# A quarter of w_out moved up in the load order, longer filler matmuls, and a planner that knows how many loads the queue holds

## The chip, the cores and the metric

The kernel runs on one core of a Trainium2 chip. The metric is the time of one execution on the device, in microseconds: 212.72 us as the median of three runs (212.54 to 212.77). The profiled execution took 212.52 us, and its trace has a span of 210.7 us from the first to the last instruction. Five engines work side by side, each in the order in which its instructions were written: TensorE (PE, matrix products), VectorE (DVE), ScalarE (ACT), GpSimd (POOL) and SyncE (SP). Loads issued from GpSimd go through one software queue of the DMA engines; SyncE has a hardware queue.

## The reference

Two stages follow each other. The first is a recurrent attention with a decaying state (4 batches, 8 heads, 768 steps, 64 columns for each head):

```python
    gamma = 1.0 - 2.0 ** (-5.0 - np.arange(H, dtype=np.float32))
    scale = 1.0 / np.sqrt(D)
    for t in range(S):
        state = gamma[None, :, None, None] * state + np.einsum('bhd,bhe->bhde', k[:, :, t], v[:, :, t])
        y[:, :, t] = scale * np.einsum('bhd,bhde->bhe', q[:, :, t], state)
```

The second takes the rows of y as 3072 tokens of 512 columns and puts them through two matrix products (w_in is 512 x 2048, w_out is 2048 x 512) with a gate between them:

```python
    h = x @ w_in
    g = h * np.cos(h)
    return (g @ w_out).astype(np.float32)
```

## The kernel before

**Tiling.** The recurrence is done in chunks of 128 steps: inside a chunk as a masked product of q and k with v, between chunks through the state. A *slot* is one chunk of two batches; there are twelve, numbered 0 to 11 in the order of `ORDER`. Two slots make a *group* of 512 tokens, and there are six groups. For one slot the work is: load q, k and v (`load`, L273); scale q and v and convert k to bf16 (`conv_q` L308, `conv_v` L312, `conv_k`); transpose q and k on TensorE (`t_mm`, L337) or, from slot 6 on, by DMA; scores (`a_mm`, L363 and L366); mask them on VectorE (`a_mask`, L372); y from the state and from the scores (`y1_mm` L428, `intra` L414, `y_first` L395); the state's update (`s_mm`, L460); and a copy of y into the token tile `xt` (`y_copy`). `copy` at L297 and L299 is a helper for all plain copies, so many different copies have its lines.

**The second stage.** A unit of the first product gives 128 columns of h for 512 tokens (`f_mm`, L472, four matmuls) or 256 columns of h for the 256 tokens of one slot (`h_mm`, L493, eight matmuls of 256 columns, called a half-width unit here). ScalarE takes the cosine (`f_cos`, L480), VectorE multiplies (`f_mul` L484, `h_mul` L501). The second product (`o_mm`, L517) adds up 128 tokens' output in one PSUM bank in four parts, part r with quarter r of w_out. PSUM has eight banks: seven go around in a list (`Banks`), one holds the state. An output block holds its bank from its first part to its last.

**Loads.** A q, k or v load of a slot is one "merged" transfer of 512 KB for both batches. In `LOADS`, "q3" is slot 3's q, "Q1" and "K1" are loads of slot 1 that convert on the way, "w1" is the second quarter of w_in (512 columns), "w0a" and "w0b" are halves of the first quarter, and "o0" to "o3" are the quarters of w_out (`load_w_out`, L289). All of them are issued by GpSimd in the order of the list (each waits for the one before to be issued). A new transfer of the queue also waits for the semaphore of the transfer eight places earlier.

**The order of the work.** For the first eight slots' loads and the first six slots' attention the order is not written by hand. `Plan` is a list scheduler that runs when the kernel is built: each operation has engines on which it may run, a cost in microseconds, operations that it follows, a rank (a small one goes first), and tokens that it takes and gives back ("bank", "cos" for the cosine buffers, "sem" for the queue's eight semaphores[...]). For loads it keeps one running time of the queue, adding size over rate and a lag for each load. `jitter` adds a random number from 0 to 4 to every rank, drawn from `SEED`. The instructions are then written in the order of the planned starts (`emit`), and the chip takes them in that order on each engine, whether or not the planned times come true. Between 4.2 and 18 us of the plan, where TensorE would have to wait longer than one filler takes, the planner puts in a filler, `idle_mm`: a matmul on zeros into a free bank, which keeps TensorE's clock up. The first seven, ahead of the plan, have 512 columns; those of the plan have 256.

**After the plan**, from about 65 us, a loop over the groups interleaves `f_mm` of one group, `o_mm` of the group before and the attention of slots 6 to 11.

The lines of the edit: the seed (L163), the engines for slot 2's scaling (`CQ` for q, `CD` for v, L589, used at L639 and L649), the token table (L592), the load list and `LAG` (L601 to L604), the merged loads' tokens (L609 to L611) and the filler given to `plan.run` (L801).

Of the kernel before, what the change touches and what calls it, by code (L numbers as in the profile page):

```python
# [29 lines left out]
class Plan:  # L30
# [16 lines left out]
    def add(self, engines, cost, fn, after=(), rank=0.0, take=(), give=(), mode=None,  # L47
            spare=0, mb=0.0, rate=0.0, lag=0.0, name=""):
        op = dict(engines=engines, cost=cost, fn=fn, after=[a for a in after if a], rank=rank,
                  take=take, give=give, mode=mode, spare=spare, mb=mb, rate=rate, lag=lag,  # L50
                  n=len(self.ops), start=None, done=None, free=None, name=name)
        self.ops.append(op)
        return op
# [106 lines left out]
            op["fn"](op["eng"])  # L160


SEED, JIT, HOLD = 41, 4.0, "PD"  # L163
HALF0, SPARE, RF, RM, COLD = 4, 1, 40.0, 40.0, 5.2


# [1 line left out]
def kernel(  # L168
# [10 lines left out]
    B, H, S, D = q.shape  # L179
# [86 lines left out]
    def load(eng, p, names):  # L266

        bp, c = divmod(ORDER[p], NC)
        for n in names.split():
            t, src = SRC[n[0].lower()]  # L270
            if len(n) == 1:
                t = (qb(p) if n == "Q" else kb(p)) if n in "QK" else t[p % PRE]
                eng.dma_start(  # L273
                    out=t.rearrange("p b h d -> p (b h) d"),
                    in_=src[ds(2 * bp, 2), :, ds(c * C, C), :].rearrange(
                        "b h t d -> t (b h) d"))
            else:
                b = int(n[1])
                eng.dma_start(
                    out=t[p % PRE][:, b],  # L280
                    in_=src[2 * bp + b, :, ds(c * C, C)].rearrange("h t d -> t h d"))

    def load_w_in(lo, n):
        nc.gpsimd.dma_start(
            out=w_in_sb[:, :, ds(lo, n)],
            in_=moe_w_in[:, ds(lo, n)].rearrange("(i p) f -> p i f", p=128))

    def load_w_out(r):
        nc.gpsimd.dma_start(  # L289
            out=w_out_sb[:, ts(r, 4), :],  # L290
            in_=moe_w_out[ts(r, 512), :].rearrange("(f p) m -> p f m", p=128))
# [252 lines left out]
    def idle_mm(e, n=1):  # L544
        bank = banks.take()
        nc.tensor.matmul(bank[:, : 256 * n].rearrange("p (n t) -> p n t", n=n),  # L546
                         lhsT=zero[:, :128], rhs=zero.unsqueeze(1).to_broadcast([128, n, 256]),
                         start=True, stop=True)
        banks.give(bank)
# [15 lines left out]
        out=dist.rearrange("p (a b) -> p a b", a=8),  # L565
# [16 lines left out]
    for i in range(7):  # L582
# [3 lines left out]
    PL = 6  # L586
    ASEP = 4
    MERGE = 4
    CQ, CD = "D", "D"  # L589
    SPLIT = {(1, 1, 0), (0, 1, 1)}  # L590
    HM, HCQ, HCV = "q2", "", ""
    plan = Plan({"bank": 7, "cos": 3, "sem": 8, "out": 4, "port": 1}, 6.5)  # L592
    add = plan.add
    SB2 = {"D": (0.33, 0.42), "A": (0.49, 0.585)}
    TT = {"D": (0.6, 0.69), "P": (1.03, 1.05)}
# [2 lines left out]
    prev = None  # L598
    at = lambda tm: dict(start=0.0, free=0.0, done=tm, lat=0.0)
    ld["q", 0, 0], ld["q", 0, 1], ld["k", 0, 0], ld["k", 0, 1] = map(at, (3.9, 5.0, 7.4, 7.4))  # L600
    LOADS = ["Q1", "K1", "v0", "v1", "w0a", "w0b", "w1", "w2", "q2", "k2", "w3a", "v2", "w3b", "q3", "k3", "v3",  # L601
             "o0", "o1", "o2", "o3", "q4", "k4", "v4", "q5", "k5", "v5", "q6", "k6", "v6",
             "q7", "k7", "v7"]
    LAG = {}  # L604
    pend = []
    for i, x in enumerate(LOADS):
        if x[0] in "qkvQK":
            p = int(x[1:])
            o = add("P", 1.2, lambda e, p=p, n=x[0]: load(nc.gpsimd, p, n),  # L609
                    [("issued", prev)] if prev else [], 50 + i if p < 7 else 45,  # L610
                    [("sem", 1)], [("sem", 1)], mb=524288e-6, rate=330e-3, name=x)  # L611
            ld[x[0].lower(), p, 0] = ld[x[0].lower(), p, 1] = o
            if p >= PRE:
                pend.append((o, x[0], p - PRE))
        elif x[0] == "w":
            r, w = int(x[1]), len(x) == 3
            lo = 512 * r + (256 if x[2:] == "b" else 0)
            o = add("P", 0.76, lambda e, lo=lo, n=256 if w else 512: load_w_in(lo, n),
                    [("issued", prev)], 50 + i, [("sem", 1)], [("sem", 1)],
                    mb=(524288e-6 if w else 1048576e-6), rate=(390e-3 if w else 415e-3),  # L620
                    lag=LAG.get(x, 0.0), name=x)
            for f in range(lo // 128, lo // 128 + (2 if w else 4)):
                ld["w", f] = o
        else:
            r = int(x[1])
            o = add("P", 0.76, lambda e, r=r: load_w_out(r), [("issued", prev)], 50 + i,
                    [("sem", 1)], [("sem", 1)], mb=1048576e-6, rate=415e-3, name=x)
            ld["o", r] = o
        prev = o
    T = {}  # L630
    G = lambda *k: T.get(k)
    for p in range(PL + 2):
        c = ORDER[p] % NC

        for b in range(2):
# [18 lines left out]
            if p < 2:  # L654
                T["cv", p, b] = add("AD"[b], SB2, lambda e, p=p, b=b: raw_v(p, b, e), [ld["v", p, b]],
                                    10 * p + 2.5 + b, [("port", 1)] if b else [], [("port", 1)] if b else [],
                                    name="rv%d%d" % (p, b))
        old = [G("a", p - NB, b) for b in range(2)] + [G("y", p - NB, b) for b in range(2)]
        if p < DMA_T:

            for u in range(2):
# [3 lines left out]
                                            name="e%s%d%d" % (x, p, u))  # L665
# [7 lines left out]
                else:  # L673
                    tq = tk = add("E", 0.45, lambda e, p=p, u=u: (t_mm(p, u, 0), t_mm(p, u, 1)),
                                  cq + ck, 10 * p + 1, [("bank", 1)], (), "full",
                                  name="t%d%d" % (p, u))
# [4 lines left out]
        else:  # L681
            for w, x in enumerate("qk"):
                T["dt", p, w] = add("S", (1.3, 4.6), lambda e, p=p, w=w: dma_t(p, w),
                                    [T["c" + x, p, 0], T["c" + x, p, 1]] + old, 10 * p,
                                    name="dt%d%d" % (p, w))
# [5 lines left out]
        elif p < ASEP:  # L691
            for u in range(2):
                T["a", p, u] = add("E", 0.225, lambda e, p=p, u=u: a_mm(p, u), kq[u], 10 * p + 2,
                                   [("bank", 2)], (), "row" if p < 2 else "quad",
                                   name="a%d%d" % (p, u))
# [4 lines left out]
        for u in range(2):  # L700
            for b in range(2):
                if (p, b, u) in SPLIT:
                    o = add("A", (0.49, 0.585), lambda e, p=p, b=b, u=u: a_save(p, b, u),
                            [T["a", p, u]], 0, (), [("bank", 1)],
                            name="ms%d%d%d" % (p, b, u))
                    T["m", p, b, u] = add("P", (1.1, 1.2), lambda e, p=p, b=b, u=u: a_late(p, b, u),
                                          [o], 0, [("port", 1)], [("port", 1)],
                                          name="ml%d%d%d" % (p, b, u))
# [16 lines left out]
        else:  # L725

            a_next = MERGE <= p < PL
            def y(e, p=p, a_next=a_next):
# [8 lines left out]
                if not a_next:  # L737
# [3 lines left out]
                    name="y%d" % p)  # L741
# [9 lines left out]
        for b in range(2):  # L751
# [4 lines left out]
                                name="yc%d%d" % (p, b))  # L756
# [8 lines left out]
        for u in units:  # L765
# [4 lines left out]
            else:  # L770
# [5 lines left out]
                     name="cos%s%d.%d" % u)  # L776
            T["mul", u] = add("D", (0.6, 0.69), mul, [c1], RM, (), [("bank", 1), ("cos", 1)],
                              name="mul%s%d.%d" % u)
# [19 lines left out]
        add("A", (0.49, 0.585), lambda e, j=j: (o_out(0, j, e), o_dma(0, j)), [T["o", j, 3]], 300, (),  # L798
            [("bank", 1)], name="oc%d" % j)
    plan.jitter(SEED, JIT)  # L800
    plan.run({"S": 2.5, "P": 3.2, "A": 5.5, "D": 3.6, "E": 4.2}, COLD, 0.6, (4.2, 18.0, 0.12, idle_mm), HOLD)  # L801
    plan.emit()

    for p in (PL + 2, PL + 3):
# [83 lines left out]
```

## Time and profile before

| what | value |
|---|---|
| time, median of 3 | 212.72 us |
| span of the trace | 210.7 us |
| TensorE clock granted | 1.00 in all stages |
| busy: TensorE, VectorE, ScalarE, GpSimd | 97%, 52%, 55%, 37% |
| bytes read and written in HBM | 27.26 MB and 6.29 MB |
| software queue | 15.47 MB written, first landing 7.05 us, last 62.44 us |
| fillers (L546) | 62, of them 55 with 256 columns |
| merged load, issue on GpSimd | 1.19 us |
| merged load, from landing to landing | 1.52 us |
| quarter of w_out, from landing to landing | 2.45 to 2.60 us |

How to read it: the shares are means over a head in which loads arrive (to 62 us) and a body in which all is loaded. Landing times of single loads are those at which the last of the sixteen landing signals of a load stands in the trace. In the views of the profile, "x8" is a count, the number after a start time is a duration in us, and brackets give the idle time of the engine ahead of the instruction, with what ended it.

### The profile page before, as it was taken

How to read it: one execution, taken by the hardware profiler on the slowest of the kernel's cores; microseconds unless marked ns; L12 is line 12 of the kernel's file. 1: busy time of each engine (PE TensorE's matmuls, PEld its weight loads, DVE VectorE, ACT ScalarE, POOL GpSimd, SP SyncE). 2: the span in 40 equal slices, each digit the busy share in tenths (PEclk: the TensorE clock that was granted, in tenths of full speed). 3: DMA queues.
4: the chain of work that ended last, by engine and by line, in shares of the span. 5: the costliest groups of instructions: out<-in, count | busy, mean ns of one | idle time of the engine just before them, and what ended most of it. 6: DMA issues, size and time to landing. Idle time of an engine off the chain costs nothing.

```text
span 210.7 us, 4885 instructions
## 1 busy us (share of the span) xinstructions
PE 203.6 (97%) x2046; PEld 111.8 (53%) x2046; DVE 109.7 (52%) x189; ACT 115.4 (55%) x193; POOL 78.0 (37%) x82
## 2 busy tenths in 40 slices
PE   7998989998999999999999999999999999999993
PEld 3776456686765545445446445445444444444462
DVE  5464999876755646537437447447442333333000
ACT  7776768387575447547547547545545554553120
POOL 8889969979998007007007007000000000000000
PEclk9999999999999999999999999999999999999999
DMA  7999999999987399999994501501101101110221
GB/s 120 202 250 235 298 323 216 215 337 344 344 259 164 103 219 240 240 208 255 117 256 143 145 30 39 151 12 56 50 3 50 50 3 50 50 50 18 84 83 68
DMA packets 57496, 32.05 MB, mean 152 GB/s; under 512 B 46593, under 2 KB 51969, under 8 KB 57473
## 3 DMA queue, kind: packets, MB, share of 16 engines
q0 software_dynamic: 14352, 15.47, 33.3%
q1 hardware_dynamic: 42976, 16.13, 30.4%
q8 instruction: 16, 0.26, 0.5%
q10 hardware_dynamic: 144, 0.13, 0.2%
q14 instruction: 8, 0.06, 0.1%
HBM read 27.26 MB, written 6.29 MB: 159 GB/s over the span
## 4 chain that ended last, share of the span: by engine, by line
PE 78%; POOL 10%; DMA 4%; issue 3%; DVE 2%; ACT 1%; POOLq 0%; DVEq 0%
PE bank L517 37%; PE bank L472 29%; DMA w_in_sb<-in_moe_w_in_dram 4%; PE bank L493 3%; POOL vf L273 3%; PE bank L366 2%; PE bank L414 2%; POOL qs L308 2%; PE bank L537 2%; PE st_ps L460 1%; PE bank L428 1%; POOL qf L273 1%; POOL vs L312 1%; POOL vx L312 1%; PE bank L337 1%
## 5 line engine op out<-in xcount | busy, mean ns | idle before, releaser
L480 ACT ACTIVATE cosb<-bank,halfpi 128x512 bf16<-128x512 f32 x96 | 65.5, 689 | 60.0 <-PE bank L472 51.4
L517 PE MATMUL bank<-w_out_sb,gt 128*128 128x512 bf16 x368 | 91.2, 379 | 0.0
L484 DVE TENSOR_TENSOR gt<-bank,cosb 128x512 bf16<-128x512 f32 x76 | 51.7, 688 | 56.2 <-ACT cosb L480 56.2
L472 PE MATMUL bank<-xt,w_in_sb 128*128 128x512 bf16 x304 | 77.0, 379 | 0.6 <-DVE am L372 0.6
L517 PEld LDWEIGHTS <-gt 128*128 128x128 bf16 x368 | 35.5, 98 | 41.9
L472 PEld LDWEIGHTS <-w_in_sb 128*128 128x128 bf16 x304 | 29.1, 98 | 34.4 <-issue 0.6
L308 POOL TENSOR_TENSOR qs<-qf,gq 128x512 bf16<-128x512 f32 x18 | 18.5, 1044 | 47.1 <-PE bank L414 47.0
L372 DVE TENSOR_TENSOR am<-bank,mask 128x512 bf16<-128x512 f32 x40 | 24.9, 680 | 0.9 <-PE bank L366 0.9
L297 ACT COPY ob<-bank 128x512 f32<-128x512 f32 (+1 forms) x24 | 13.9, 578 | 15.7 <-PE bank L517 14.5
L312 POOL TENSOR_TENSOR vs<-vf,gk 128x512 bf16<-128x512 f32 x20 | 20.7, 1047 | 0.3
L493 PE MATMUL bank<-xt,w_in_sb 128*128 128x256 bf16 x160 | 18.6, 273 | 0.9 <-DMA w_in_sb<-in_moe_w_in_dram 0.6
L501 DVE TENSOR_TENSOR gt<-bank,cosb 128x512 bf16<-128x512 f32 x20 | 13.6, 689 | 8.2 <-ACT cosb L480 7.9
L493 PEld LDWEIGHTS <-w_in_sb 128*128 128x128 bf16 x160 | 15.4, 98 | 3.8 <-DMA w_in_sb<-in_moe_w_in_dram 0.8
L297 ACT CAST xt<-bank 128x512 bf16<-128x512 f32 x24 | 12.9, 589 | 8.0 <-PE bank L414 7.3
L297 ACT CAST ks<-kf 128x512 bf16<-128x512 f32 x20 | 11.5, 622 | 2.5 <-DMA vf<-in_v_dram 2.5
L299 DVE CAST stb<-st_ps 128x512 bf16<-128x512 f32 x10 | 6.9, 688 | 11.1 <-PE st_ps L460 11.1
L546 PE MATMUL bank<-zero 128*128 128x256 bf16 (+1 forms) x62 | 11.2, 320 | 1.2 <-DVE halfpi L562 1.1
L273 POOL DMA_DIRECT2D vf<-in_v_dram x8 | 9.5, 1187 | 0.0
L414 PE MATMUL bank<-am,vs 64*64 64x64 bf16 (+1 forms) x320 | 8.2, 205 | 0.1
L546 PEld LDWEIGHTS <-zero 128*128 128x128 bf16 x62 | 6.1, 106 | 4.0 <-issue 2.0
L297 ACT COPY qkt<-bank 128x512 bf16<-128x512 bf16 x12 | 6.6, 587 | 2.1 <-PE bank L337 2.1
L273 POOL DMA_DIRECT2D kf<-in_k_dram x6 | 7.1, 1182 | 1.6 <-issue 1.6
(60 smaller groups left out, 107.9 us busy)
## 6 DMA issues: line engine op xcount, KB each, us to landing
out_dram<-ob SPq DMA_DIRECT2D x23, 256.0 KB, 2.1
vf<-in_v_dram POOLq DMA_DIRECT2D x8, 512.0 KB, 9.2
qf<-in_q_dram POOLq DMA_DIRECT2D x6, 512.0 KB, 10.6
kf<-in_k_dram POOLq DMA_DIRECT2D x6, 512.0 KB, 10.1
w_out_sb<-in_moe_w_out_dram POOLq DMA_DIRECT2D x4, 512.0 KB, 13.8
qf<-in_q_dram SPq DMA_DIRECT2D x4, 512.0 KB, 4.7
kf<-in_k_dram SPq DMA_DIRECT2D x4, 512.0 KB, 6.2
vf<-in_v_dram SPq DMA_DIRECT2D x4, 512.0 KB, 6.1
```

What stands on the lines that cost most here:

```text
L273: eng.dma_start(out=t.rearrange("p b h d -> p (b h) d"), in_=src[ds(2 * bp, 2), :, ds(c * C, C), :].rearrange("b h t d -> t (b h) d"))
L297: nc.scalar.copy(out=out, in_=in_)
L308: ENG[e].tensor_tensor(out=qb(p)[:, b], in0=qf[p % PRE][:, b], in1=bc(gq, ORDER[p] % NC), op=ALU.mult)
L312: ENG[e].tensor_tensor(out=vb(p)[:, b], in0=vf[p % PRE][:, b], in1=bc(gk, ORDER[p] % NC), op=ALU.mult)
L372: nc.vector.tensor_tensor(out=am[p % 2][b][u], in0=bank.rearrange("p (a t) -> p a t", a=HP), in1=(dec[:, b] if p < 2 else mask.unsqueeze(1 ...
L472: nc.tensor.matmul(bank, lhsT=w_in_sb[:, i, ts(f, 128)], rhs=xt[g % 2][:, i, :], start=(i == 0), stop=(i == KIN - 1))
L480: nc.scalar.activation(out=cb, in_=bank, func=AF.Sin, bias=halfpi)
L484: nc.vector.tensor_tensor(out=gt[g % 2][:, f, :], in0=bank, in1=cb, op=ALU.mult)
L493: nc.tensor.matmul(bank[:, ts(e, 256)], lhsT=w_in_sb[:, i, ts(f + e, 128)], rhs=xt[g % 2][:, i, ts(hf, 256)], start=(i == 0 and e == 0), s ...
L501: nc.vector.tensor_tensor(out=gt[g % 2][:, f : f + 2, ts(hf, 256)], in0=bank.rearrange("p (f t) -> p f t", f=2), in1=cb.rearrange("p (f t) ...
L517: nc.tensor.matmul(bank, lhsT=gt[g % 2][:, f, ts(j, 128)], rhs=w_out_sb[:, f, :], start=(f == 0), stop=(f == KOUT - 1))
L546: nc.tensor.matmul(bank[:, : 256 * n].rearrange("p (n t) -> p n t", n=n), lhsT=zero[:, :128], rhs=zero.unsqueeze(1).to_broadcast([128, n, ...
```

## The change

The edits, all in the planned part:

1. o0, the first quarter of w_out, is loaded after w3b and ahead of q3, k3 and v3, in place of after them, so that output matmuls can be used earlier to fill TensorE's time.
2. The planner has a new token "ring" of seven. Every q, k or v load takes one and gives it back at its landing, so that the plan never has more than seven of these loads on the way. It stands for the room that the software queue has.
3. The scaling of slot 2's v goes from VectorE to GpSimd.
4. A filler has 512 columns and a planned length of 0.225 us, in place of 256 columns and 0.12 us.
5. The planner adds a lag of 0.15 us to w1, and so to all that lands after it.
6. The seed of the random ranks is 60 in place of 41, and with the other edits this gives a new order of everything in the plan.

```diff
-SEED, JIT, HOLD = 41, 4.0, "PD"
+SEED, JIT, HOLD = 60, 4.0, "PD"
...
-    CQ, CD = "D", "D"
+    CQ, CD = "D", "P"
...
-    plan = Plan({"bank": 7, "cos": 3, "sem": 8, "out": 4, "port": 1}, 6.5)
+    plan = Plan({"bank": 7, "cos": 3, "sem": 8, "out": 4, "port": 1, "ring": 7}, 6.5)
...
-    LOADS = ["Q1", "K1", "v0", "v1", "w0a", "w0b", "w1", "w2", "q2", "k2", "w3a", "v2", "w3b", "q3", "k3", "v3",
-             "o0", "o1", "o2", "o3", "q4", "k4", "v4", "q5", "k5", "v5", "q6", "k6", "v6",
+    LOADS = ["Q1", "K1", "v0", "v1", "w0a", "w0b", "w1", "w2", "q2", "k2", "w3a", "v2", "w3b", "o0", "q3", "k3", "v3",
+             "o1", "o2", "o3", "q4", "k4", "v4", "q5", "k5", "v5", "q6", "k6", "v6",
              "q7", "k7", "v7"]
-    LAG = {}
+    LAG = {"w1": 0.15}
...
-                    [("sem", 1)], [("sem", 1)], mb=524288e-6, rate=330e-3, name=x)
+                    [("sem", 1), ("ring", 1)], [("sem", 1), ("ring", 1)], mb=524288e-6, rate=330e-3, name=x)
...
-    plan.run({"S": 2.5, "P": 3.2, "A": 5.5, "D": 3.6, "E": 4.2}, COLD, 0.6, (4.2, 18.0, 0.12, idle_mm), HOLD)
+    plan.run({"S": 2.5, "P": 3.2, "A": 5.5, "D": 3.6, "E": 4.2}, COLD, 0.6, (4.2, 18.0, 0.225, lambda e: idle_mm(e, 2)), HOLD)
```

## The prediction

> **What bounds the kernel now.** I read the busy shares first, then the busy time by stage, then the order of instructions on TensorE and GpSimd in the stage that the change touches.
>
> ```profile
> PE 203.6 (97%) x2046; PEld 111.8 (53%) x2046; DVE 109.7 (52%) x189; ACT 115.4 (55%) x193; POOL 78.0 (37%) x82
> ```
>
> TensorE is busy for 97% of the span, so an average leaves little to win. The table by stage (columns: stretch, its length, then busy time and count of each engine) says where the rest is.
>
> ```profile
> 0.00:17.16 17.16, 15.44 (x166) 10.51 (x167) 8.71 (x29) 13.20 (x27) 14.80 (x21) 1.00 1.40 192
> 17.16:26.00 8.84, 8.84 (x67) 5.25 (x68) 6.89 (x11) 6.09 (x11) 8.82 (x10) 1.00 1.18 277
> 26.00:36.00 10.00, 9.07 (x154) 5.57 (x152) 9.71 (x19) 7.52 (x14) 8.08 (x9) 1.00 1.17 274
> 36.00:49.00 13.00, 13.00 (x189) 10.16 (x187) 9.87 (x16) 8.55 (x15) 11.35 (x11) 1.00 1.14 281
> 49.00:64.00 15.00, 14.32 (x142) 9.39 (x139) 9.20 (x16) 9.99 (x18) 14.91 (x16) 1.00 0.93 302
> 64.00:207.00 143.00, 142.89 (x1337) 70.92 (x1336) 64.88 (x99) 70.06 (x112) 20.05 (x20) 1.00 0.42 107
> ```
>
> From 64 us to the end TensorE never rests (142.89 of 143), at the full clock, and nothing there is edited. What is before 17 us is filled with dummy matmuls (L546) while the first quarter of w_in comes in. So all that can be won or lost is TensorE idle time between 16 and 64 us. The order of time on TensorE shows it; the brackets give the idle time and what ended it:
>
> ```profile
> 17.16 2.79 PE L493 MATMUL bank<-xt,w_in_sb 128*128 128x256 bf16 x24 [0.55 <-DMA w_in_sb<-in_moe_w_in_dram]
> ...
> 30.43 1.89 PE L472 MATMUL bank<-xt,w_in_sb 128*128 128x512 bf16 x8 [0.62 <-DVE am L372]
> ...
> 35.77 1.03 PE L493 MATMUL bank<-xt,w_in_sb 128*128 128x256 bf16 x8 [0.30 <-ACT xt L297]
> ...
> 50.23 0.40 PE L337 MATMUL bank<-ident,qs 128*128 128x128 bf16 x4 [0.68 <-POOL qs L308]
> ```
>
> These are four stalls, 0.55 + 0.62 + 0.30 + 0.68 = 2.15 us. Each understates the loss by about 0.16 us, because a matmul is drawn longer than it holds the array (a 512-column one is drawn 379 ns, yet the next starts 216 ns after it). So the true loss is 0.71 + 0.78 + 0.46 + 0.84 = **2.8 us**, and the floor is 212.72 - 2.8 = 209.9.
>
> The cause of the last stall is on GpSimd:
>
> ```profile
> 42.99 1.19 POOL L273 DMA_DIRECT2D qf<-in_q_dram  x1
> 45.75 1.15 POOL L273 DMA_DIRECT2D kf<-in_k_dram  x1 [1.56 <-issue]
> 46.92 1.06 POOL L308 TENSOR_TENSOR qs<-qf,gq 128x512 bf16<-128x512 f32 x1
> 47.90 1.19 POOL L273 DMA_DIRECT2D vf<-in_v_dram  x1
> 49.12 1.05 POOL L308 TENSOR_TENSOR qs<-qf,gq 128x512 bf16<-128x512 f32 x1
> ```
>
> GpSimd sits 1.56 us in front of the load k6 though no semaphore holds it. From the landing signals in the trace, q4, k4, v4, q5, k5, v5 and q6 are in flight then, seven merged loads; q4 lands at 45.41 and k6 goes at 45.75. So an eighth merged load doesn't fit. Behind k6 wait both halves of the scaling of q4 (46.92 and 49.12), and TensorE waits for the second. q4 itself was there at 45.41.
>
> **What the Trainium skill says.** "DMA: Bandwidth & Descriptors", section "SWDGE vs HWDGE vs iDMA": GpSimd computes the descriptors of its own DMAs and appends them to rings which the DMA engines drain, with one queue. It names no capacity; the trace gives seven. "TensorE: Matmul & The Clock Gate", section "Wait — 56ns, not 53.3ns?": 512 columns go every 426.7 ns cold and 215.7 ns warm. The trace agrees (427 ns between the first fillers, 216 ns later). Its section "What's actually happening" has the clock fall only after an idle window of about 3.4 us; stalls of up to 0.84 us here leave it at 1.00. "GPSIMD Engine Reference", section 3.1, measures a two-input tensor_tensor at 1.96 times VectorE's time; here it is 1055 ns (L312 POOL) against 684 ns (L312 DVE), 1.54 times, and I use these.
>
> **The change, part by part.**
>
> *Ring token.* Only the written order changes. The planner holds an eighth merged load back until one has landed, so on GpSimd the scaling of q4, with a better rank than any load, goes before k6. Both halves then take 45.4 + 2 x 1.05 = 47.5, against 50.2 before; k4 lands at 47.3 and ScalarE's conversion takes two times 0.6, so the transposes can start at about 48.6 instead of 50.23. This removes the last stall: 0.84 us. k6, v6 and the loads of slot 7 go later, but seven loads are queued at 1.52 us apart, over 10 us of work, so the queue doesn't run dry.
>
> *Scaling of v for slot 2 to GpSimd.* VectorE loses 2 x 0.684, drawn as 1.28 us at 28.50. This is just ahead of the masks at 29.70 that hold TensorE's bank; VectorE is busy 9.71 of 10 us in that stage, and two cosine products (their cosines end by 28.24) wait until 32.09. In the freed 1.2 us they or the masks go earlier and free the bank: 0.78 us, at least 0.3. GpSimd gains 2 x 1.055 = 2.1 us. Its order shows it waiting there for queue semaphores, 0.31 + 0.78 + 0.77 = 1.86 us:
>
> ```profile
> 26.78 0.75 POOL L289 DMA_DIRECT2D w_out_sb<-in_moe_w_out_dram  x1 [0.31 <-DMA w_in_sb<-in_moe_w_in_dram]
> 28.30 0.74 POOL L289 DMA_DIRECT2D w_out_sb<-in_moe_w_out_dram  x1 [0.78 <-DMA vf<-in_v_dram]
> 29.81 1.17 POOL L273 DMA_DIRECT2D qf<-in_q_dram  x1 [0.77 <-DMA w_in_sb<-in_moe_w_in_dram]
> ```
>
> v2 lands at 28.02, so both halves are scaled by 30.2 to 31, ahead of the last mask (32.2 before, some 31.6 then) that y2 needs as well. The rest, 0.25 us, falls into the time in which q3 is not there yet. Cost nothing.
>
> *First quarter of w_out ahead of slot 3.* The software queue is serial and full from 6 to 62 us: a merged load lands every 1.52 us, a quarter of a weight every 2.55. The load ahead of it, w3b, lands at 29.28, so o0 lands at 29.28 + 2.55 = 31.8 instead of 36.35, and q3, k3, v3 each 2.55 later: 33.3, 34.9, 36.4. Everything from q4 on lands as before. The four first parts of the output matmuls, 4 x 0.865 = 3.5 us, can now fill the wait at 35.24 for xt of slot 2: gain 0.46 us. Does slot 3's delay open a hole? Its transposes move from 34.4 to about 36.5, its y from 41.1 to about 43.6, its half-width units from 43.5 to about 46. What TensorE can do from 34 to 46 without slot 3: eight half-width units of slot 2 (7.0 us), parts 0 and 1 of the output (6.9 us, o1 lands at 38.8), and slot 3's own transposes and scores (about 2.5 us): 16.4 us for 12. No hole if the plan uses them; up to 2.55 us if it leaves slot 3 where it was. An output part holds one bank of seven until o3 lands at 43.9, which can cost a bank wait: 0 to 0.6 us, the size of the bank wait above.
>
> *Fillers.* The 55 single fillers become some 27 of 512 columns. Until 14.83, when the first half of w_in's quarter lands, TensorE has nothing else to finish; an overshoot is at most 0.22 us and lies ahead of that. In the cold part (to 5.1 us) it can be 0.43, ahead of k's landing at 7.05. Cost nothing; at most 0.1 at the hand-over.
>
> *Lag of w1 by 0.15, and the seed.* No instruction of their own. w1 and what follows landed 0.1 to 0.7 us after the sum that the planner's rates give; the lag halves this. w0b, whose miss (17.11) makes the first stall, is ahead of w1: this stall I leave in, 0.71 us. The seed draws all ranks again, so near ties fall anew; the same model left four stalls of 0.7 us in mean, and I allow for one such new stall: 0 to 2.8, taken 0.7.
>
> **Sum.** 0.84 + 0.78 + 0.46 = 2.1 won, 0.7 lost: 212.72 - 1.4 = **211.3 us**.
>
> **Rivals.** (A) All four stalls go and none comes; the first goes if the half-width unit of slot 1 on the landed half is written ahead of the one that waits for w0b: 209.9. For it: everything needed is in flight early. Against: the w0b miss isn't treated. 0.13. (B) The stalls only move: each released engine meets another late transfer, GpSimd (14.91 of 15 us busy from 49 to 64) above all; 2.1 won, 2.1 lost, 212.7. 0.15. (C) Slower: slot 3's 2.55 us shows as a hole on TensorE, while the GpSimd and VectorE repairs give 0.84 + 0.78: 212.72 + 2.55 - 1.6 = 213.7. For it: TensorE takes its work in the written order, and a landing that is later than planned stops it at once. Against: 16.4 us of other work for 12. 0.22. The forecast has the remaining 0.50.
>
> **Range and chances.** 210.2 to 213.3 holds the forecast with its new stalls of 0 to 1.4, B, and the smaller half of C; it leaves out most of A and the rest of C. Faster: the forecast, A and a third of B, 0.68; same: most of B, 0.11; slower: 0.21.
>
> **What would show it.** Right: no GpSimd idle ahead of k6, the scaling of q4 starting by 46 us; no wait of L472 for a mask near 30 us; output matmuls (L517) already near 34 us; L312 on GpSimd alone; idle of TensorE from 17 to 64 us about 1.4 us, and the same last 143 us. Wrong: TensorE waiting for slot 3's transposes or evictions at 36 to 44, a wait for a bank held by an output part, or a new GpSimd wait near 50 to 60.

## The result and the profile after

The changed kernel takes 210.11 us (209.84 to 210.40) against 212.63 us before: a ratio of 0.9885 with a 95% interval from 0.9865 to 0.9906, so 2.5 us faster, with 2.0 to 2.9 us inside the interval. The forecast was 211.3, with a range from 210.2: the direction and the place were right, the gain was larger than the range allowed. The two profiled executions differ by 2.12 us (212.52 and 210.40), and what follows in traces accounts for this.

The table by stage of the changed kernel (stretch, length, then busy time and count of TensorE, weight loads, VectorE, ScalarE, GpSimd; then clock and DMA):

```profile
17.16:26.00 8.84, 8.70 (x66) 4.82 (x64) 7.01 (x11) 6.39 (x11) 8.82 (x9) 1.00 1.19 276
26.00:36.00 10.00, 10.00 (x150) 5.95 (x149) 8.99 (x16) 7.86 (x14) 8.69 (x10) 1.00 1.16 274
36.00:49.00 13.00, 13.00 (x202) 10.90 (x201) 10.65 (x18) 9.32 (x16) 12.87 (x13) 1.00 1.14 278
49.00:64.00 15.00, 15.00 (x228) 10.06 (x227) 7.61 (x14) 10.21 (x20) 14.94 (x15) 1.00 1.08 324
```

From 26 to 64 us TensorE is now busy all the time; before, 9.07 of 10 and 14.32 of 15. The same four places in the order of time on TensorE carry no bracket any more, which means no idle time ahead of them:

```profile
16.78 2.78 PE L493 MATMUL bank<-xt,w_in_sb 128*128 128x256 bf16 x24
...
29.67 1.90 PE L472 MATMUL bank<-xt,w_in_sb 128*128 128x512 bf16 x8
...
33.88 1.03 PE L517 MATMUL bank<-w_out_sb,gt 128*128 128x512 bf16 x4
34.74 2.78 PE L493 MATMUL bank<-xt,w_in_sb 128*128 128x256 bf16 x24
...
49.91 0.39 PE L337 MATMUL bank<-ident,qs 128*128 128x128 bf16 x4
```

Measured from the start of one matmul to the start of the next, less what this step takes undisturbed, the four stalls of before were 0.71, 0.69, 0.47 and 0.84 us, 2.7 together. The changed kernel has none of them; it has 0.30 us ahead of the first full-width unit at 19.7, which waits for w1, its first half-width unit starts 0.22 us later, and the longer filler behind this unit takes 0.1 us more. The balance is 2.7 - 0.6 = 2.1 us. Nearly all of it lies behind 29 us, as the scores of slot 2 show, before and then after:

```profile
29.02 0.79 PE L366 MATMUL bank<-qkt 64*64 64x128 bf16 x32
```

```profile
28.95 0.79 PE L366 MATMUL bank<-qkt 64*64 64x128 bf16 x32
```

TensorE gets there only 0.07 us earlier. The first stall of 0.71 us is gone, but the new losses of 0.6 us lie in the same stretch, so the gain is that of the other three stalls: 0.69 + 0.47 + 0.84 = 2.0 us. On GpSimd the first half of q4's scaling starts at 46.05 with no wait in front of it or of k6, and the second half still stands behind k6:

```profile
44.89 1.15 POOL L273 DMA_DIRECT2D qf<-in_q_dram  x1
46.05 1.06 POOL L308 TENSOR_TENSOR qs<-qf,gq 128x512 bf16<-128x512 f32 x1
47.04 1.19 POOL L273 DMA_DIRECT2D kf<-in_k_dram  x1
48.25 1.06 POOL L308 TENSOR_TENSOR qs<-qf,gq 128x512 bf16<-128x512 f32 x1
```

### The profile page after: what moved, and what is told of

The parts are those of the page before. It is cut to its first block, busy times and chain, and to the rows that moved or that the text cites. A ratio compares the mean times of both kernels' runs of the same rounds, so it can differ in the third digit from the quotient of the medians.

```text
span 208.5 us, 4822 instructions
## 1 busy us (share of the span) xinstructions
PE 203.3 (97%) x2017; PEld 108.9 (52%) x2017; DVE 107.8 (52%) x186; ACT 116.1 (56%) x194; POOL 80.1 (38%) x84
## 4 chain that ended last, share of the span: by engine, by line
PE 91%; DMA 6%; POOL 1%; DVE 0%; ACT 0%; issue 0%; DVEq 0%; POOLq 0%
PE bank L517 38%; PE bank L472 32%; PE bank L493 7%; DMA w_in_sb<-in_moe_w_in_dram 4%; PE bank L366 3%; PE bank L337 2%; PE bank L414 2%; PE st_ps L460 2%; PE bank L537 2%; PE bank L428 2%; DMA qf<-in_q_dram 1%; PE bank L546 1%; POOL am L384 1%; PE bank L363 0%; ACT gt L380 0%; DVE qs L299 0%
## 5 line engine op out<-in xcount | busy, mean ns | idle before, releaser
L517 PE MATMUL bank<-w_out_sb,gt 128*128 128x512 bf16 x368 | 91.1, 379 | 0.0
L517 PEld LDWEIGHTS <-gt 128*128 128x128 bf16 x368 | 35.6, 98 | 42.3
L312 POOL TENSOR_TENSOR vs<-vf,gk 128x512 bf16<-128x512 f32 x22 | 22.7, 1045 | 1.6 <-DMA vf<-in_v_dram 1.4
L297 ACT COPY ob<-bank 128x512 f32<-128x512 f32 (+1 forms) x24 | 13.9, 578 | 15.4 <-PE bank L517 14.2
L493 PEld LDWEIGHTS <-w_in_sb 128*128 128x128 bf16 x160 | 15.4, 98 | 2.6
L546 PE MATMUL bank<-zero 128*128 128x512 bf16 x33 | 10.6, 448 | 1.1 <-DVE halfpi L562 1.1
L297 ACT COPY qkt<-bank 128x512 bf16<-128x512 bf16 x13 | 7.1, 594 | 2.7 <-PE bank L337 2.4
L366 PE MATMUL bank<-qkt 64*64 64x128 bf16 x320 | 7.2, 218 | 0.0
```

The source lines that it names most:

```text
L297: nc.scalar.copy(out=out, in_=in_)
L312: ENG[e].tensor_tensor(out=vb(p)[:, b], in0=vf[p % PRE][:, b], in1=bc(gk, ORDER[p] % NC), op=ALU.mult)
L366: nc.tensor.matmul(ap[b][ts(x, 64), a, :], lhsT=kt(n, b, h)[:, ts(x, 64)], rhs=qt(n, b, h), tile_position=(64 * b, 64 * x), skip_group_che ...
L493: nc.tensor.matmul(bank[:, ts(e, 256)], lhsT=w_in_sb[:, i, ts(f + e, 128)], rhs=xt[g % 2][:, i, ts(hf, 256)], start=(i == 0 and e == 0), s ...
L517: nc.tensor.matmul(bank, lhsT=gt[g % 2][:, f, ts(j, 128)], rhs=w_out_sb[:, f, :], start=(f == 0), stop=(f == KOUT - 1))
```

## The experiments

The additive account of the forecast (each stall has its own cure, the cures add up) stands against a second one that the traces after suggest: several engines are late at the same place, so one cure alone shows the next wait. "Ratio" is against the kernel before on the same chip; all medians of before lie between 212.53 and 212.80 us.

| kernel | us | ratio (95% interval) |
|---|---|---|
| changed kernel | 210.11 | 0.9885 (0.9865 to 0.9906) |
| changed, fillers as pairs of 256 | 210.24 | 0.9893 (0.9871 to 0.9916) |
| before, fillers fused | 212.56 | 0.9997 (0.9987 to 1.0007) |
| before, two units swapped | 212.40 | 0.9992 (0.9983 to 1.0001) |
| before, q4 scaled first | 211.75 | 0.9957 (0.9940 to 0.9974) |
| before, q4 scaled first, units swapped | 211.57 | 0.9945 (0.9927 to 0.9962) |
| before, v2 on GpSimd | 212.66 | 1.0005 (0.9995 to 1.0016) |
| before, all four of these | 211.96 | 0.9972 (0.9963 to 0.9981) |
| before, o0 issued early | 214.84 | 1.0110 (1.0095 to 1.0125) |
| before, k3 converted late, q4 first | 212.39 | 0.9991 (0.9982 to 1.0000) |
| the same, units swapped | 212.27 | 0.9985 (0.9976 to 0.9995) |
| changed, o0 back | 210.73 | 0.9922 (0.9909 to 0.9935) |
| changed, o0 back, k3 converted late | 210.60 | 0.9918 (0.9894 to 0.9941) |
| changed, v2 on VectorE | 212.18 | 0.9979 (0.9969 to 0.9990) |
| changed, seed 41 | 215.75 | 1.0141 (1.0107 to 1.0175) |
| before with seed 60, o0, v2 alone | 210.34 | 0.9888 (0.9872 to 0.9904) |
| changed, beside it | 210.39 | 0.9887 (0.9869 to 0.9904) |
| changed, state first (two runs) | 210.33, 210.49 | 0.9900, 0.9890 |

**The ring token** changes nothing in the changed kernel. With it taken out, the planner writes the same instructions in the same order on every engine. It is not without effect in itself: the token and the move of slot 2's v to GpSimd each bring a half of q4's scaling ahead of k6 in the written order, and with both taken out of the changed kernel the planner puts both halves behind k6. GpSimd of the kernel with the token and with v2 on VectorE (below) waits for q4 in front of its scaling, and no more in front of k6:

```profile
45.94 1.04 POOL L308 TENSOR_TENSOR qs<-qf,gq 128x512 bf16<-128x512 f32 x1 [1.00 <-DMA qf<-in_q_dram]
46.93 1.19 POOL L273 DMA_DIRECT2D kf<-in_k_dram  x1
```

**The first stall: w0b.** Two kernels keep their plan and change only how fillers are written, one swaps two units in the written order.

```diff
 fillers as pairs (changed kernel)
-... (4.2, 18.0, 0.225, lambda e: idle_mm(e, 2)), HOLD)
+... (4.2, 18.0, 0.225, lambda e: (idle_mm(e), idle_mm(e))), HOLD)
 fillers fused (before): of each two fillers the first has 512 columns, the second is left out
-... (4.2, 18.0, 0.12, idle_mm), HOLD)
+... (4.2, 18.0, 0.12, fused), HOLD)
 units swapped (before): after plan.run
+    for n in ("%s", "cos%s", "mul%s"):
+        a, b = by[n % "h0.2"], by[n % "h1.0"]
+        a["start"], b["start"] = b["start"], a["start"]
```

> The changed kernel with the same plan and order, but each filler of 512 columns written as two of 256, so TensorE has 26 more matmuls and weight loads ahead of the first half-width units. Theory (order): the first stall is gone because the unit of slot 1 on w0a is written ahead of the unit that needs w0b, so a late w0b costs nothing; the time stays within 0.3 us of the changed kernel, 210.1. Rival (instruction fetch): TensorE's 16 KB instruction fetch, at 15.9 us after the change and 14.5 before, moves back to about 14.5, holds up one DMA engine by some 1 us, w0b lands near 17.1, and 0.4 to 0.7 us come back: 210.5 to 210.8.

> The kernel before with the same plan and order, but its fillers fused in pairs into fillers of 512 columns, so TensorE has some 27 fewer matmuls and weight loads. If the instruction fetch makes w0b late, the fetch moves from 14.5 to about 15.9 us, w0b lands near 16.4 in place of 17.1 and the first stall of 0.71 us shrinks to 0.1 or less: 212.0. If w0b's landing has another cause, it stays at 17.1 and the time at 212.6.

> The kernel before with the half-width unit of slot 1 on w0a written ahead of the unit of slot 0 that needs w0b, cosine and product with it, nothing else. If the order of these two makes the first stall, 0.7 us go: 211.9, and w0b may still land at 17.1. If something else holds TensorE there, no change: 212.6.

With the fillers as pairs TensorE's instruction fetch comes at 15.1 us in place of 15.9 and w0b lands at 17.11 in place of 16.38, and the time is the same: the unit of slot 1 on w0a now stands in front, so a late w0b costs nothing. With the fillers fused before, the fetch moves from 14.5 to 15.8, w0b lands at 16.38 and the stall is gone from the trace, as expected, and yet the time doesn't move. In that trace k3 lands at 32.82 in place of 32.31, and the wait for xt near 35 us is longer by 0.76 us, more than the stall that went:

```profile
36.22 1.03 PE L493 MATMUL bank<-xt,w_in_sb 128*128 128x256 bf16 x8 [1.06 <-ACT xt L297]
```

The swap gives 0.2 us (0 to 0.4). So both cures work on the stall and hardly on the time: most of what is won at 17 us is lost later.

The stall itself isn't a fixed cost. The kernels "q4 scaled first", "o0 issued early" and "v2 on GpSimd" have the head of the kernel before unchanged, and their traces show 0.32 us, 0.34 us and nothing at this place, against 0.55 us before.

**The last stall: GpSimd.**

```diff
 q4 scaled first (before): after plan.run
+    by["cq40"]["start"] = by["k6"]["start"] - 0.02
+    by["cq41"]["start"] = by["k6"]["start"] - 0.01
```

> The kernel before with both halves of the scaling of q4 issued on GpSimd ahead of the loads k6 and v6, the order on all other engines the same. Theory: the stall of 0.84 us at 49.3 goes, 211.8. Rival: the stall moves, because k6, v6 and slot 4's v come later and a transfer or a conversion ends just as late: 212.6. The full queue then shows as an idle time ahead of the scaling of q4, not ahead of k6.

> The kernel before with the scaling of q4 ahead of k6 and v6, and the units of slots 0 and 1 swapped; the conversion of k3 in its old place. If that conversion takes up what the swap gives: no more than 0.2 us faster than the scaling edit alone (211.75), 211.5 to 211.8, and TensorE's wait near 35 us grows from 0.46. If the terms add up: 211.1.

The scaling edit alone gives 0.9 us (0.6 to 1.3), the whole of the 0.84 us stall; the wait for q4 moves in front of its scaling, and TensorE no longer waits at 49 us:

```profile
45.66 2.03 POOL L308 TENSOR_TENSOR qs<-qf,gq 128x512 bf16<-128x512 f32 x2 [1.36 <-DMA qf<-in_q_dram]
```

It is the one term of the forecast that holds by itself. The swap on top of it gives 0.2 us more, which is inside the intervals; in that run w1 landed at 20.18, and TensorE waited 0.58 us for it in place of w0b.

**The stall near 30 us: v2 on GpSimd, and all four together.**

```diff
 v2 on GpSimd (before): after plan.run
+    for b in range(2):
+        T["cd", 2, b]["eng"] = "P"
```

> The kernel before with the scaling of slot 2's v on GpSimd, the written order else the same. As forecast (terms add up): the bank wait of 0.78 us near 30 us goes, 211.8. New theory (one wait behind several stalls): ScalarE's conversion of k3 stands in its order ahead of two cosines and of slot 2's copies into xt, and waits for k3's landing near 32.3; TensorE reaches the half-width units of slot 2 earlier and then waits for xt until about 35.7 all the same: 212.4 to 212.6.

> The kernel before with four edits of written order or engine and no new plan: fillers fused in pairs, the units of slots 0 and 1 swapped, slot 2's v scaled on GpSimd, q4 scaled ahead of the loads k6 and v6. If the terms add up: 212.6 - 0.7 - 0.8 - 0.84 = 210.2, the changed kernel's time. If k3's landing takes up the first two: 212.6 - 0.84 - 0.2 = 211.5 to 211.8, with a longer wait of TensorE for xt near 35 us, 1.3 to 1.9 us in place of 0.46.

Nothing is won alone, and the four together give no more than the scaling edit (0.6 us against 0.9; the intervals overlap). The trace of the kernel with only v2 moved shows why, GpSimd first and then TensorE:

```profile
34.59 1.05 POOL L308 TENSOR_TENSOR qs<-qf,gq 128x512 bf16<-128x512 f32 x1
```

```profile
30.29 1.89 PE L472 MATMUL bank<-xt,w_in_sb 128*128 128x512 bf16 x8 [0.42 <-DVE am L372]
35.70 0.40 PE L337 MATMUL bank<-ident,qs 128*128 128x128 bf16 x4 [1.27 <-POOL qs L308]
```

The bank wait at 30 us only fell from 0.62 to 0.42. The second half of q3's scaling starts at 34.59 in place of 33.20, and TensorE waits 1.27 us for it. Not all of this 1.4 us is due to the two added operations: GpSimd was already some 0.4 us late in this run, and in two other runs that were as late (q4 scaled first with the swap, and with k3 late) the scaling starts at 33.73 and 33.81, so some 0.8 us is theirs. "Cost nothing" was wrong for the old order. This trace has no stall at 17 us and none at 49 us, and the time is that of before all the same: the wait at 35 us takes the place of both. A second wait lies at the same place; ScalarE of the kernel before:

```profile
32.38 1.14 ACT L297 CAST ks<-kf 128x512 bf16<-128x512 f32 x2 [2.45 <-DMA vf<-in_v_dram]
33.48 1.27 ACT L480 ACTIVATE cosb<-bank,halfpi 128x512 bf16<-128x512 f32 x2
34.64 1.07 ACT L297 CAST xt<-bank 128x512 bf16<-128x512 f32 x2
```

ScalarE stands 2.45 us in front of the conversion of k3. (The view names a v load, but what landed at 32.31 is k3.) Behind it in order are two cosines and slot 2's copies into xt, so TensorE can't have the next half-width unit before about 35.7 in this order, however early it comes.

**Is it k3's conversion alone?** A rule for the planner puts it behind the copies, once with and once without the swap, both with q4 scaled first.

```diff
 k3 converted late (before): ahead of plan.jitter
+    for b in range(2):
+        T["ck", 3, b]["after"] += [("issued", T["yc", 2, 1])]
```

> The kernel before with the scaling of q4 ahead of k6 and v6 and the rule that k3's conversion follows slot 2's copies into xt, planned anew with the old seed. Against the scaling edit alone (211.75) the wait near 35 us goes or shrinks: 211.3 to 211.7, if nothing new comes at the hand-over near 62 to 72 us, where this plan has a gap of 0.8 us; with it 212.0.

> The same with the units of slots 0 and 1 swapped as well. If k3's conversion was what took up the swap's gain, the swap now counts: 0.4 to 0.7 us faster than the same kernel without it. If another wait takes it up: within 0.2 us.

No: this is 0.6 to 0.7 us slower than the scaling edit alone, and the swap still gives only 0.1 us. With k3 out of the way TensorE waits at the same place, longer, and for a third engine:

```profile
33.72 1.04 PE L472 MATMUL bank<-xt,w_in_sb 128*128 128x512 bf16 x4
35.96 1.25 PE L493 MATMUL bank<-xt,w_in_sb 128*128 128x256 bf16 x10 [1.20 <-DVE gt L484]
```

VectorE's products, which free the banks, stand behind v2's scaling, the masks and the copy of the state. So at 35 to 36 us TensorE was held up by each of the three other engines in turn: 1.06 us by ScalarE (fillers fused), 1.27 us by GpSimd (v2 moved) and 1.20 us by VectorE (k3 late). That this one place takes up what is won before it is the reading that fits all these kernels; no run treats all three waits at once in the old order.

**o0.** Once only its issue is moved in the old order, once it is taken back in the new, without and with the rule for k3.

```diff
 o0 issued early (before): after plan.run
+    by["o0"]["start"] = by["q3"]["start"] - 0.01
 o0 back (changed kernel)
-    ... "w3b", "o0", "q3", "k3", "v3", "o1", ...
+    ... "w3b", "q3", "k3", "v3", "o0", "o1", ...
```

> The kernel before with o0 issued ahead of q3, k3 and v3, the written order of all else the same, so slot 3's loads land 2.5 us later and nothing is put in the gap. If the landing of k3 sets when TensorE goes on near 35.7 us: 2.3 to 2.6 us slower, 215.0, with a wait of 2.5 to 3 us there. If TensorE has that much slack there: 212.6 to 213.5.

> The changed kernel with o0 back behind v3, planned anew with all other edits. If moving o0 is what keeps the conversion of k3 out of the way (its k3 lands 2.5 us later, and an output part fills the time): the plan has one conversion of k3 ahead of xt again, and 0.3 to 1.0 us come back, 210.5 to 211.2. If the other edits carry the gain: 210.1 to 210.3.

> The changed kernel with o0 back behind v3 and one rule more for the planner: the conversion of k3 on ScalarE comes after slot 2's copies into xt. If the order on ScalarE is what counts and o0's move only brings it about: the wait near 34 us (0.64 us with o0 back alone) shrinks to 0.2 or less and the time falls from 210.7 to 210.1 or 210.3. If the output part that o0's early landing allows is needed as filling: it stays at 210.6 to 210.8.

In the old order the move costs 2.3 us. TensorE waits for the scaling of q3 and then for xt, and after these gaps its clock is halved:

```profile
36.66 0.40 PE L337 MATMUL bank<-ident,qs 128*128 128x128 bf16 x4 [2.22 <-POOL qs L308]
...
38.10 1.65 PE L493 MATMUL bank<-xt,w_in_sb 128*128 128x256 bf16 x8 [0.38 <-ACT xt L297]
```

```profile
39.00:40.00 1.00, 1.00 (x16) 0.53 (x18) 0.37 (x1) 0.27 (x2) 0.98 (x2) 0.50 1.25 207
```

The granted clock (the third number from the end) is 0.50 from 38.4 to 41.8 us, which for a busy TensorE is a loss of up to 1.7 us (half of 3.4, an estimate). The stall at 49 us doesn't show in this trace, so a part is taken back. Only a plan that knows of the move puts other work there. In the new plan taking it back costs 0.8 us (0.37% of 212.6), one conversion of k3 is ahead of xt again, and TensorE waits for xt:

```profile
34.74 1.03 PE L493 MATMUL bank<-xt,w_in_sb 128*128 128x256 bf16 x8 [0.47 <-ACT xt L297]
```

With the rule for k3 the wait there is 0.24 us, now for a bank that VectorE frees, and the time 210.6, between the two; the intervals don't separate it from either. Whether order or filling is the larger part of o0's 0.8 us stays open.

**The edits out of the changed kernel, and three of them alone.**

```diff
 v2 on VectorE: -    CQ, CD = "D", "P"   +    CQ, CD = "D", "D"
 seed 41:       -    SEED, JIT, HOLD = 60, 4.0, "PD"   +    SEED, JIT, HOLD = 41, 4.0, "PD"
 three alone: the kernel before with SEED 60, CD = "P" and o0 ahead of q3
```

> The changed kernel with slot 2's v scaled on VectorE again, planned anew. If GpSimd's taking it removes the wait for a bank near 30 us: the wait of some 0.7 to 1.0 us is back there, and since k3's conversion is out of the way now it is not taken up later: 210.8 to 211.1. If that wait is hidden by other work: 210.1 to 210.3.

> The changed kernel with the seed of before, 41. If the gain is the edits' and not the draw's: within 0.4 us of 210.1, with no stall over 0.5 us. If the draw carries it: 211 or more.

> The kernel before with three of the edits alone: seed 60, o0 moved, slot 2's v on GpSimd; no ring token, no lag, fillers of 256. Its plan has the same order as the changed kernel's on every engine except that the unit that needs w0b is again ahead of slot 1's unit on w0a. If the three carry the gain and the rest is the swap: the wait for w0b of 0.5 to 0.7 us is back and is not taken up later, 210.6 to 210.9. If the swap is worth nothing here either: 210.1 to 210.3. If lag or ring token matter: over 211.

> The changed kernel as it is, beside the others on one chip: 210.1 to 210.3 by every theory.

v2 back on VectorE costs 2.0 us, twice what I expected: the bank wait is back, and the other order also waits 0.69 us at 65.1 within slot 4's y, and in this run 0.47 us for w1:

```profile
30.75 1.89 PE L472 MATMUL bank<-xt,w_in_sb 128*128 128x512 bf16 x8 [0.62 <-DVE am L372]
```

The seed was a miss altogether: I expected no difference, and it costs 5.5 us. Up to 64 us that kernel is nearly as good as the changed one; then the output parts are used up and slot 5's y stands alone on TensorE:

```profile
70.66 0.30 PE L414 MATMUL bank<-am,vs 64*64 64x128 bf16 x8 [0.98 <-DVE am L372]
71.25 0.27 PE L414 MATMUL bank<-am,vs 64*64 64x128 bf16 x5 [0.30 <-DVE am L372]
...
73.78 0.59 PE L472 MATMUL bank<-xt,w_in_sb 128*128 128x512 bf16 x1 [0.69 <-ACT xt L297]
```

```profile
64.00:75.00 11.00, 8.37 (x209) 5.01 (x210) 4.93 (x9) 4.26 (x8) 4.73 (x5) 0.89 0.75 130
```

TensorE is busy 8.37 of 11 us, and the mean granted clock is 0.89 there: it is 0.50 from 72.7 to 76.1 us, after the gaps. The fastest of this kernel's six executions (214.22 us) has a mean clock of 0.998 and the slowest (216.59 us) one of 0.984, so by this reading the gaps cost some 4 us by themselves and the halved clock up to 2.4 us more. In the changed kernel five output parts (20 matmuls, 63.60 to 68.02) lie between slot 4's and slot 5's y and hide the masks:

```profile
63.60 4.49 PE L517 MATMUL bank<-w_out_sb,gt 128*128 128x512 bf16 x20
68.02 0.42 PE L428 MATMUL bank<-qkt,stb 64*64 64x128 bf16 x16
```

The three edits alone, beside the changed kernel on one chip, are as fast (0.9888 and 0.9887). Longer fillers, lag and ring token are worth nothing that can be measured, within about 0.3 us.

**A try at a better one.** The changed kernel with slot 0's state update ahead of the unit that waits for w1:

```diff
 state first (changed kernel): after plan.run
+    by["s0"]["start"] = by["f0.4"]["start"] - 0.01
```

> The changed kernel with slot 0's state update (16 small matmuls, 0.37 us) written ahead of the first full-width unit, which waits 0.30 us for w1. If w1's landing is all that holds TensorE at 19.3 us: 0.2 to 0.3 us faster than the changed kernel, 209.8 to 209.9. If the scaled v of slot 0 (GpSimd to 19.2) or the bank comes later than w1: 210.1 or a little more.

> The changed kernel with the state update of slot 0 ahead of the first full-width unit, again, for a comparison on one chip: 0.1 to 0.3 us faster than the changed kernel if the 0.3 us wait for w1 is filled by it; equal if the wait moves behind.

It is no faster: 210.49 against 210.39 on one chip. In that run of the changed kernel w1 was on time and there was nothing to fill.

## Why the forecast was wrong, point by point

- **What bounds the kernel: right.** All that was won is TensorE's idle time between 16 and 64 us, all four stalls went, and the floor of 209.9 was nearly reached. Three of the four make up the gain. The new signs came as written: L517 at 33.88, the scaling of q4 at 46.05, L312 on GpSimd alone.
- **The sum: this is the failed step.** "2.1 won" held: the three stalls that it names were 2.0 us in the trace. What failed is the term "0.7 lost", one new stall of the mean size of the four old ones, set beside the first stall left in at 0.71. So the forecast kept 1.4 us of stalls; the trace has 0.30, 0.22 and 0.1 us (the longer filler) in the head and none behind it, 0.6 together. That is 0.8 of the 1.1 us between the forecast gain of 1.4 and the measured one of 2.5; the rest is inside the interval. Two things can have removed the stall for w0b: the swap that rival A names, which the longer filler brings (after a filler of 0.225 us both units are ready in the plan, after 0.12 us only the one that waits for w0b), and w0b's landing at 16.38. The kernel with three edits has neither (old order of the two units, w0b at 17.32) and is as fast: slot 1's y came 0.64 us later there (15.75 against 15.11), and w0b was just in time:

```profile
17.36 2.79 PE L493 MATMUL bank<-xt,w_in_sb 128*128 128x256 bf16 x24
```

  So I priced as a stall of its own what is part of the loads' pace in the head, which differs from run to run: two executions of the kernel "state first" reach this unit at 16.82 and 17.36. Rival A, at 0.13, was nearly the case that came (all four stalls went, small ones came), and the range left out most of it.
- **The ring token: right in kind, not needed here.** The GpSimd stall and its worth were right (0.9 us by the scaling edit). But beside the other edits the token changes no instruction, since v2's scaling on GpSimd brings the same order, which the forecast did not see. And only one half of q4's scaling goes ahead of k6, not both: the second ends at 49.3 in place of the forecast 47.5, which is still in time for TensorE at 49.91.
- **v2 on GpSimd: right in its place, wrong in "cost nothing".** Alone in the old order it delays q3's scaling by some 0.8 us and wins nothing; in a plan made anew it is free, with o0 moved and also with o0 back, where q3's second half is scaled at 32.89 and TensorE doesn't wait for it. Its 2 us in the new plan were also not foreseen.
- **Terms that add up: wrong.** Four edits worth 2.3 us on paper gave 0.6 us. In the old order the stalls at 17, 30 and 35 us act as one lateness seen three times: near 35 us one engine or another holds TensorE up when it comes earlier. That "2.1 won" came true in the new plan is thus in part luck: its three cures were priced one by one in the old order, where v2's is worth nothing and o0's costs 2.3 us.
- **o0: right that there is no hole with a new plan, and rival C's size came true in the old order, by luck.** It measured 2.3 us against 2.55, but the sum is another one: longer waits, a halved clock that the forecast did not reckon with, and a stall that went. The forecast quoted an idle window of about 3.4 us for a fall of the clock; here the longest gap ahead of the fall was 2.4 us, with 1.3 us of work in the last 3.4, and the measurement decides.
- **"Nothing there is edited" after 64 us: wrong.** The plan reaches to about 70 us, and with the old seed the hand-over alone loses several us. I had called the seed an edit without instructions of its own; together with o0 and v2 it is needed for the gain. What the seed or o0 does alone in a new plan of the kernel before was not run and stays open.

## What to carry to other kernels

Stalls on the bound engine are not separate accounts: before adding up their cures, look at what every other engine has ready at the last of them, since one late place downstream takes back all that is won ahead of it. In a kernel whose order a planner writes, an edit's worth is that of the new order, so compare the written orders first (an edit may change none), and look at the hand-over to the next stage, where work used up too early leaves a bare dependency chain. A gap of 2 us on TensorE can cost more than itself, so look at the granted clock behind it.

## What the runs showed of the hardware

- TensorE's instructions come in transfers of 16 KB that take about 0.9 to 1.1 us of one DMA engine (that they are TensorE's is read from their moving with its fillers alone). The first falls at 14.5 to 15.3 us with fillers of 256 columns and at 15.4 to 16.3 us with fillers of 512, and in most runs the last of the sixteen landing signals of the loads behind it comes 0.3 to 1.4 us after the fifteenth, for several loads in a row. In the kernel before this was w0b (fifteenth 16.03, last 17.11); in the profiled run of the changed kernel w1 (18.90 and 19.66).
- The software queue takes seven merged loads of 512 KB; the eighth waited 1.56 us with no semaphore to wait for, until the first had landed. In all four traces with this wait k6 goes 0.33 to 0.34 us after q4's landing, whether the wait was 0.47 or 2.33 us.
- After gaps TensorE's granted clock was 0.50 for 3.4 us in two kernels (38.4 to 41.8 with o0 issued early, 72.7 to 76.1 with seed 41), with 1.3 and 1.9 us of work in the 3.4 us ahead. With 2.1 us of work in such a stretch (v2 on GpSimd, a gap of 1.27 us) it stayed at 1.00.
